# Row maxima of the segment units: whole rows with the causal mask added in VectorE's reduction, in place of blocks with separately masked diagonals

## The chip, the cores and the metric

The kernel runs on one core of a Trainium2 chip. The metric is the device time of one execution in microseconds (us), from the first to the last instruction of the program with what lies around them. The core's engines work side by side and in order, each on its own queue: TensorE (PE in the profile; PEld is its loading of weights), VectorE (DVE), ScalarE (ACT), GpSimd (POOL) and SyncE (SP, which here only issues transfers).

## The reference

Two attentions over the same sequence length (2048 tokens, 512 features, 32 heads of 16) are mixed by a gate. Cut to what matters:

```python
# side A: full softmax attention, no mask
scores = einsum("bhqd,bhkd->bhqk", q, k) * scale
p = softmax(scores); o = einsum("bhqk,bhkd->bhqd", p, v);  a = o @ wo
# side B: four segments of 512 tokens, causal inside a segment, plus a linear memory of earlier ones
mask = (ar[:, None] < ar[None, :]) * (-1e9)
for s in range(4):
    logits = einsum(qs, ks) * scale + mask
    a_dot = softmax(logits) @ vs
    o = g * (phi(qs) @ M) / (phi(qs) @ z + 1e-6) + (1 - g) * a_dot
    M, z = M + phi(ks).T @ vs, z + sum(phi(ks))
b = concat(o) @ wo_b
out = gate * a + (1 - gate) * b          # gate = sigmoid(x . gate_w)
```

The softmax needs, for each query and head, the maximum of its scores before the exponential. This kernel computes these maxima in a pass of products of their own; the change is in that pass, on side B.

## The kernel before

A first stage (to about 327 us) projects x to q, k and v, both sides, and builds the memory terms. The main stage then goes through 64 **units**: a unit is a side, a group of 4 heads and a chunk of 512 queries. A units have 64 slots and B units ("segment units") 10; they alternate, so that a pair has 74 slots, and there are 32 pairs, 2368 slots in all. In every slot `n` of the main stage TensorE does, in this order:

- `score_part(n)` (line 660): one product of up to 512 columns into one of three PSUM banks `st`; ScalarE takes the exponential of it into `p` (line 683).
- `max_part(n + LEAD, bank)` with LEAD = 96 (line 208 through `max_product`): a product into one of four PSUM banks `sm0` to `sm3`, taken in turn, for a unit that comes later; VectorE reduces it to maxima. The list `maxs` says which part each slot does: among the 64 parts of an A unit the 10 parts of a B unit are spread, one every seventh slot (`start, apart = 6, 7`; in the second unit pair and the last one every third slot).
- After every third slot (`BURST = 3`): the products with v of earlier slots (`some_values`, line 716), or products with the output weights in their place (line 793). So TensorE's order of work is three score products and three maximum products in one **burst**, then the products with v, then the next burst; here that is called a **group**.

The score product and the maximum product of a slot use different halves of the array's rows (heads 0 and 1 lie in partitions 0 to 63, heads 2 and 3 from 64), and `maxs` is laid out so that the two of a slot are on opposite halves.

A maximum part on side A is one product of 128 queries by 512 keys for one head and one `tensor_reduce` of the bank (line 223). A B unit needs, for each of 4 heads and 4 blocks `s` of 128 queries, the maximum over the keys up to the query. Before the change its 10 parts are, for each pair `r` of heads:

- `i` = 0 and 1: four products of 128 columns in one bank, the diagonal blocks of two query blocks for two heads. ScalarE copies the bank to `dg` (line 234), GpSimd replaces what lies above the diagonal (line 235), and eight slots later (`MASK_T`) VectorE reduces `dg` (line 238). The bank is free once ScalarE has copied it.
- `i` = 2 and 3: for one head the blocks left of the diagonal of query block 1 (128 columns) and of block 3 (384 columns): two products, one reduction by blocks (line 244).
- `i` = 4: the same of query block 2 for both heads (256 columns each): two products, one reduction (line 248).

In all that is 28 products, each with a load of weights, in 10 slots. `finish_max` then reduces the partial maxima to `nm` (line 180 for A, 182 for B), GpSimd splits it in two (`ms`, lines 187 and 188), and `transpose_max` (lines 196 to 202) turns it on TensorE, copies it on ScalarE and sends it by DMA into rows 48 and 49 of the unit's q, where the score product subtracts it. `todo` and `late` hold the slots at which these steps are issued: the steps of an A unit's `finish_max` are issued right after its last part, its transpose 14 slots after; a B unit's 9 and 18 slots after.

All orders are written out by hand; the waits between engines are put in when the program is built, from the tiles that each instruction reads and writes.

## Time and profile before

| | us |
|---|---|
| median of 3 runs | 1882.21 |
| lowest and highest | 1882.15 and 1885.49 |
| the profiled execution, its own time | 1883.44 |
| its span, first to last instruction | 1881.7 |

TensorE's granted clock is 1.0 of full speed over the span. Busy shares of the span: PE 99%, DVE 85%, ACT 80%, PEld 53%, POOL 17%. In the stretch from 450 to 1700 us the DVE is busy for 1207.2 of 1250 us.

Rows of groups read: line, engine, operation, tiles out<-in, shapes, count | busy us in all, mean ns of one | idle time of the engine just before, and what ended it. Rows of a timeline read: start in us from the span's start, us from the first start to the last end of the merged instructions, engine, line, operation, tiles, count. VectorE's instructions overlap at their ends, so that the next may start before the row's duration is over.

### The profile page before, as it was taken

The page shows a single profiled execution, that of the slowest core. Times are in us where ns is not written, and L with a number is a line of the kernel's source. Part 1 is how long each engine was busy: PE and PEld are TensorE (multiplying, and loading weights), DVE is VectorE, ACT ScalarE, POOL GpSimd, SP SyncE. Part 2 cuts the span into 40 slices and gives each one's busy share as a digit, 9 for nine tenths or more (in the row PEclk, how much of TensorE's full clock was granted, in tenths as well). Part 3 has the DMA queues.
Part 4 walks back from the last instruction along what each step waited for, and adds up shares of the span by engine and source line. Part 5 has one row for each costly group of instructions (what it writes and reads, how often), then busy time and mean ns, then how long its engine had stood idle before and what let it go on. Part 6 is the DMA issues. An engine that isn't in the chain of part 4 may idle for free.

```text
span 1881.7 us, 46459 instructions
## 1 busy us (share of the span) xinstructions
PE 1863.1 (99%) x18153; PEld 1006.1 (53%) x18153; DVE 1596.5 (85%) x2745; ACT 1502.9 (80%) x2900; POOL 314.9 (17%) x515
## 2 busy tenths in 40 slices
PE   9999999999999999999999999999999999999998
PEld 7888676555555454444444444444444454555545
DVE  4235777999999999999999999999999999999820
ACT  5445444898888898888888888888888888888884
POOL 3001222111111111121111111211121211111210
PEclk9999999999999999999999999999999999999999
DMA  7567555234343433343434343434343434343211
GB/s 239 192 231 255 196 184 192 84 115 136 87 109 86 115 91 111 94 117 97 117 92 117 98 113 102 113 98 113 97 113 101 113 103 115 102 114 95 84 57 46
DMA packets 124170, 227.31 MB, mean 121 GB/s; under 512 B 34952, under 2 KB 49960, under 8 KB 123440
## 3 DMA queue, kind: packets, MB, share of 16 engines
q1 hardware_dynamic: 122448, 222.68, 41.1%
q8 instruction: 144, 2.36, 0.5%
q0 software_dynamic: 1216, 1.14, 0.2%
q14 instruction: 74, 0.61, 0.1%
q10 hardware_dynamic: 288, 0.52, 0.1%
HBM read 155.52 MB, written 67.52 MB: 119 GB/s over the span
## 4 chain that ended last, share of the span: by engine, by line
PE 90%; ACT 4%; DMA 3%; DVE 1%; issue 1%; SPq 1%; POOL 1%; ACTq 0%; POOLq 0%; DVEq 0%
PE ops L716 30%; PE st L660 27%; PE sm L208 14%; PE pr L320 11%; PE ops L793 6%; ACT p L683 2%; ACT dg L234 1%; DMA qB<-mt 1%; PE num L502 1%; POOL mn L380 1%; SPq L202 0%; DMA qdB<-q 0%; PE sm L793 0%; PE mps L533 0%; DMA raw<-wqkv 0%
## 5 line engine op out<-in xcount | busy, mean ns | idle before, releaser
L683 ACT ACTIVATE p<-st 128x512 f32<-128x512 f32 x2304 | 1223.4, 605 | 180.8 <-PE sm L208 147.4
L223 DVE TENSOR_REDUCE pm<-sm 128x1 f32<-128x512 f32 x2048 | 1282.9, 683 | 62.1 <-PE sm L208 43.0
L208 PE MATMUL sm<-kA,qA 48*128 48x512 f32 x2048 | 741.5, 445 | 0.0
L660 PE MATMUL st<-qA,kA 50*128 50x512 f32 x2048 | 693.6, 436 | 3.6 <-ACT p L683 3.1
L660 PEld LDWEIGHTS st<-qA,kA 50*128 50x128 f32 x2048 | 332.9, 185 | 436.0 <-ACT p L683 370.6
L716 PE MATMUL ops<-p,vA 128*17 128x512 f32 (+3 forms) x5848 | 556.4, 469 | 0.0
L208 PEld LDWEIGHTS sm<-kA,qA 48*128 48x128 f32 x2048 | 332.5, 184 | 21.1 <-DVE pm L223 7.9
L716 PEld LDWEIGHTS ops<-p,vA 128*17 128x17 f32 x5848 | 109.7, 95 | 174.0 <-issue 152.4
L208 PE MATMUL sm<-kB,qB 48*128 48x128 f32 (+2 forms) x896 | 168.6, 291 | 0.0
L208 PEld LDWEIGHTS sm<-kB,qB 48*128 48x128 f32 x896 | 134.6, 186 | 9.8 <-DVE pm L223 2.8
L235 POOL TENSOR_SCALAR_AFFINE_SELECT dg<-dg 128x512 f32<-128x512 f32 x128 | 81.2, 635 | 289.1 <-ACT dg L234 289.1
L660 PE MATMUL st<-qB,kB 50*128 50x384 f32 (+3 forms) x512 | 120.4, 341 | 2.6 <-DMA qB<-mt 1.2
L187 POOL CAST ms<-nm 128x16 fp32r<-128x16 f32 x64 | 12.6, 196 | 646.6 <-DVE nm L180 401.5
L383 DVE TENSOR_TENSOR q<-full,q 128x512 fp32r<-128x512 f32 x64 | 44.1, 689 | 86.9 <-ACT q L376 86.4
L660 PEld LDWEIGHTS st<-qB,kB 50*128 50x128 f32 x512 | 71.4, 185 | 67.9 <-ACT p L683 47.3
L664 POOL TENSOR_SCALAR_AFFINE_SELECT p<-p 128x512 f32<-128x512 f32 x128 | 78.8, 634 | 95.9 <-ACT p L683 93.9
L244 DVE TENSOR_REDUCE pmB<-sm 128x4 f32<-128x512 f32 x128 | 87.3, 682 | 0.5 <-PE sm L208 0.5
L716 PE MATMUL ops<-p,vB 128*17 128x128 f32 (+3 forms) x1192 | 86.5, 398 | 0.4
L238 DVE TENSOR_REDUCE pmB<-dg 128x4 f32<-128x512 f32 x128 | 86.7, 677 | 0.0
L375 ACT COPY full<-pr 128x512 f32<-128x512 f32 x64 | 37.3, 583 | 52.0 <-PE pr L320 51.8
L234 ACT COPY dg<-sm 128x512 f32<-128x512 f32 x128 | 76.4, 597 | 1.0 <-DVE pmB L238 0.6
L767 DVE RECIPROCAL rec<-rec 128x32 f32<-128x32 f32 x44 | 15.1, 344 | 66.0 <-DMA rec<-odA 35.3
(145 smaller groups left out, 1588.8 us busy)
## 6 DMA issues: line engine op xcount, KB each, us to landing
kA<-kdA SPq DMA_DIRECT2D x256, 128.0 KB
vA<-vdA SPq DMA_DIRECT2D x31, 544.0 KB
kA<-kdA SPq DMA_DIRECT2D x256, 64.0 KB
qdA<-q SPq DMA_DIRECT2D x32, 256.0 KB
kdA<-q SPq DMA_DIRECT2D x32, 256.0 KB
qdB<-q SPq DMA_DIRECT2D x32, 256.0 KB
qA<-qdA SPq DMA_DIRECT2D x64, 128.0 KB
kdB<-q SPq DMA_DIRECT2D x32, 256.0 KB
```

The source lines that it names most:

```text
L208: nc.tensor.matmul(ps[:, n0:n0 + n], rows(qt[u][:, :, s * 128:(s + 1) * 128], h, 48), rows(k[:, :, k0:k0 + n], h, 48), start=True, stop=True)
L223: nc.vector.tensor_reduce(pm[:, h, s, kc:kc + 1], ps, axis=AX.X, op=ALU.max)
L234: nc.scalar.copy(dg, blocked(ps))
L235: nc.gpsimd.affine_select(out=dg, in_=dg, pattern=[[0, 4], [-1, 128]], base=0, channel_multiplier=1, compare_op=ALU.is_ge, fill=MASKED)
L238: todo.append((m + MASK_T, lambda: nc.vector.tensor_reduce(to, dg.rearrange("p (h s) t -> p h s t", h=2), axis=AX.X, op=ALU.max)))
L244: nc.vector.tensor_reduce(pm[:, 1, h, 3:7], blocked(ps), axis=AX.X, op=ALU.max)
L320: nc.tensor.matmul(ps, l(a, k), r(b, k), start=(n == 0), stop=(n == 11))
L660: nc.tensor.matmul(ps[:, n0:n0 + CH - q0], rows(k[:, :, b * 128:(b + 1) * 128], h, 50), rows(q[:, :, q0:], h, 50), start=True, stop=True)
L664: nc.gpsimd.affine_select(out=x, in_=x, pattern=[[0, 4], [1, 128]], base=0, channel_multiplier=-1, compare_op=ALU.is_ge, fill=0.0)
L683: nc.scalar.activation(p[:, h], ps, AF.Exp, scale=SCALE)
L716: nc.tensor.matmul(ops[32 * h:32 * h + 17, q0:q0 + 128 * w], v[:, 17 * h:17 * h + 17], p[:, h, c0:c0 + 128 * w], start=(i == 0), stop=done ...
L793: nc.tensor.matmul(ps[32 * t:32 * t + 32, 128 * (j % (ps.shape[1] // 128)):128 * (j % (ps.shape[1] // 128)) + 128], held[side, c][:, o, 12 ...
```

## The change

A B unit's maxima are taken in whole rows: for a head and a query block `s`, one product over all 128 (s + 1) keys up to and with the diagonal block, and one VectorE instruction that adds a mask, kept in SBUF, takes the smallest of the negated sums, and writes it out as the negated maximum. The mask is zero but for its last 128 columns, in which the part above the diagonal is -3.0e38. So there are 16 products and 16 reductions in place of 28 products, 10 reductions from banks or copies, 4 copies on ScalarE and 4 selects on GpSimd. The 10 slots stay: per pair of heads two slots hold a row block of 128 and one of 384 columns, one slot two of 256, and two slots one of 512. In a slot with two, the order of issue is product, reduction, product, reduction, both in the same bank.

B's `finish_max` no longer reduces, and is issued right after the last part; transposes are issued 8 slots after an A unit's last part and 12 after a B unit's. The mask is built by GpSimd at the start of the main stage, behind the loads of the gates.

```diff
-MASKED = -1.0e9 / SCALE
-MASK_T = 8
...
-    pmB = [mp.tile([128, 2, 4, 8], F32, name=f"pmB{i}", bufs=1) for i in range(2)]
-    for t in pmB:
-        nc.gpsimd.memset(t, -3.0e38)
-
     def finish_max(u):
-        nm = mp.tile([128, 4, 4], F32, tag="nm", name="nm")
-        pm = pmt.pop(u)
+        nm = pmt.pop(u)
         if u[0] == "A":
+            pm, nm = nm, mp.tile([128, 4, 4], F32, tag="nm", name="nm")
             nc.vector.tensor_reduce(nm, pm, axis=AX.X, op=ALU.max, negate=True)
-        else:
-            nc.vector.tensor_reduce(nm.rearrange("p h (a b) -> p (h a) b", b=2),
-                                    pm.rearrange("p b h (a k) -> p (h a) b k", a=2), axis=AX.X, op=ALU.max, negate=True)
...
             k = kt_[u, c]
-            h0 = 2 * r
-            if i < 2:
...
-                dg = dp.tile([128, 4, 128], F32, tag="dg", name="dg")
-                nc.scalar.copy(dg, blocked(ps))
-                nc.gpsimd.affine_select(out=dg, in_=dg, pattern=[[0, 4], [-1, 128]], base=0, channel_multiplier=1,
-                                        compare_op=ALU.is_ge, fill=MASKED)
...
+            for h, s in (((0, 0), (0, 2)), ((0, 1), (1, 1)), ((1, 0), (1, 2)), ((0, 3),), ((1, 3),))[i]:
+                w = 128 * (s + 1)
+                n0 = 128 * (s == 2) + 256 * (s == 1 and h)
+                max_product(ps, u, 2 * r + h, s, n0, w, k)
+                nc.vector.tensor_tensor_reduce(out=tri["rest"][:, 0:w], in0=ps[:, n0:n0 + w], in1=tri["mask"][:, CH - w:],
+                                               scale=-1.0, scalar=3.0e38, op0=ALU.add, op1=ALU.min,
+                                               accum_out=pm[:, 2 * r + h, s:s + 1])
         if m == last_max[u]:
             def finish():
-                late.append((m + MASK_T + 2 + LATE_T - (4 if side == "A" else 0), u, finish_max(u)))
-            todo.append((m + (MASK_T + 1 if side == "B" else 0), finish))
+                late.append((m + LATE_T + (4 if side == "B" else 0), u, finish_max(u)))
+            todo.append((m, finish))
...
+    tri["rest"] = dp.tile([128, CH], F32, name="rest")
+    tri["mask"] = dp.tile([128, CH], F32, name="mask")
+    nc.gpsimd.memset(tri["mask"], 0.0)
+    nc.gpsimd.affine_select(out=tri["mask"][:, 384:], in_=tri["mask"][:, 384:], pattern=[[-1, 128]], base=0, channel_multiplier=1,
+                            compare_op=ALU.is_ge, fill=-3.0e38)
```

More of the change, by code (lines that the diff above doesn't have):

```diff
@@ L167, in gated_mix @@
     pmt = {}
+    tri = {}
     todo = []
     late = []
-    pmB = [mp.tile([128, 2, 4, 8], F32, name=f"pmB{i}", bufs=1) for i in range(2)]
-    for t in pmB:
-        nc.gpsimd.memset(t, -3.0e38)
     def finish_max(u):
-        nm = mp.tile([128, 4, 4], F32, tag="nm", name="nm")
-        pm = pmt.pop(u)
+        nm = pmt.pop(u)
         if u[0] == "A":
+            pm, nm = nm, mp.tile([128, 4, 4], F32, tag="nm", name="nm")
             nc.vector.tensor_reduce(nm, pm, axis=AX.X, op=ALU.max, negate=True)
-        else:
-            nc.vector.tensor_reduce(nm.rearrange("p h (a b) -> p (h a) b", b=2),
-                                    pm.rearrange("p b h (a k) -> p (h a) b k", a=2), axis=AX.X, op=ALU.max, negate=True)
         ms = mp.tile([128, 2, 2, 2, 4], F32R, tag="ms", name="ms")
@@ L202, in transpose_max @@
                 nc.sync.dma_start(raw(qt[u])[64 * r + 48:64 * r + 50], raw(mt)[32 * i + 16 * r:32 * i + 16 * r + 16])
-    def blocked(ps):
-        return ps.rearrange("p (b t) -> p b t", t=128)
     def max_product(ps, u, h, s, n0, n, k, k0=0):
@@ L215, in max_part @@
         if u not in pmt:
-            pmt[u] = mp.tile([128, 4, 4, 4], F32, tag="pmA", name="pm") if side == "A" else pmB[(c * NG + g) % 2]
+            pmt[u] = mp.tile([128, 4, 4] + [4] * (side == "A"), F32, tag="pm" + side, name="pm")
         pm = pmt[u]
@@ L227, in max_part @@
             k = kt_[u, c]
-            h0 = 2 * r
-            if i < 2:
-                for n in range(4):
-                    b = i + 2 * (n % 2)
-                    max_product(ps, u, h0 + n // 2, b, 128 * n, 128, k, 128 * b)
-                dg = dp.tile([128, 4, 128], F32, tag="dg", name="dg")
-                nc.scalar.copy(dg, blocked(ps))
-                nc.gpsimd.affine_select(out=dg, in_=dg, pattern=[[0, 4], [-1, 128]], base=0, channel_multiplier=1,
-                                        compare_op=ALU.is_ge, fill=MASKED)
-                to = pm[:, i, h0:h0 + 2, 3::4] if i == 0 else pm[:, i, h0:h0 + 2, 1::6]
-                todo.append((m + MASK_T, lambda: nc.vector.tensor_reduce(
-                    to, dg.rearrange("p (h s) t -> p h s t", h=2), axis=AX.X, op=ALU.max)))
-            elif i < 4:
-                h = h0 + i - 2
-                max_product(ps, u, h, 1, 0, 128, k)
-                max_product(ps, u, h, 3, 128, 384, k)
-                nc.vector.tensor_reduce(pm[:, 1, h, 3:7], blocked(ps), axis=AX.X, op=ALU.max)
-            else:
-                for f in range(2):
-                    max_product(ps, u, h0 + f, 2, 256 * f, 256, k)
-                nc.vector.tensor_reduce(pm[:, 0, h0:h0 + 2, 4:6], ps.rearrange("p (h b t) -> p h b t", h=2, b=2), axis=AX.X,
-                                        op=ALU.max)
+            for h, s in (((0, 0), (0, 2)), ((0, 1), (1, 1)), ((1, 0), (1, 2)), ((0, 3),), ((1, 3),))[i]:
[5 more added lines that the diff above has]
+                                               accum_out=pm[:, 2 * r + h, s:s + 1])
         if m == last_max[u]:
             def finish():
-                late.append((m + MASK_T + 2 + LATE_T - (4 if side == "A" else 0), u, finish_max(u)))
-            todo.append((m + (MASK_T + 1 if side == "B" else 0), finish))
+                late.append((m + LATE_T + (4 if side == "B" else 0), u, finish_max(u)))
+            todo.append((m, finish))
     def run_todo(m):
@@ L602, in gated_mix @@
     va = ctx.enter_context(tc.tile_pool(name="va", bufs=2, reuse_waits="tile"))
-    dp = ctx.enter_context(tc.tile_pool(name="dp", bufs=3, reuse_waits="tile"))
+    dp = ctx.enter_context(tc.tile_pool(name="dp", bufs=1, reuse_waits="tile"))
     ob = ctx.enter_context(tc.tile_pool(name="ob", bufs=2, reuse_waits="tile"))
```

## The prediction

> **What bounds the kernel now.** I read the page first: busy shares, the slices of the span, the chain that ended last.

> ```profile
> PE 1863.1 (99%) x18153; PEld 1006.1 (53%) x18153; DVE 1596.5 (85%) x2745; ACT 1502.9 (80%) x2900; POOL 314.9 (17%) x515
> PE   9999999999999999999999999999999999999998
> DVE  4235777999999999999999999999999999999820
> PE 90%; ACT 4%; DMA 3%; DVE 1%; issue 1%; SPq 1%; POOL 1%; ACTq 0%; POOLq 0%; DVEq 0%
> ```

> TensorE is never idle and carries 90% of the chain; VectorE is the second nearest, nearly full in the main stage. So a weight load saved is worth something, and so is anything that holds TensorE. How near the two are is read from the timeline, one group of TensorE and then VectorE beside it.

> ```profile
> 829.15 0.50 PE L660 MATMUL st<-qA,kA 50*128 50x512 f32 x1
> 829.15 0.73 PE L208 MATMUL sm<-kA,qA 48*128 48x512 f32 x2
> 829.49 0.63 PE L660 MATMUL st<-qA,kA 50*128 50x512 f32 x2
> 829.73 0.40 PE L208 MATMUL sm<-kA,qA 48*128 48x512 f32 x1
> 830.06 1.05 PE L716 MATMUL ops<-p,vA 128*17 128x512 f32 x8
> 831.04 0.50 PE L660 MATMUL st<-qA,kA 50*128 50x512 f32 x1
> ```
> ```profile
> 829.72 3.85 DVE L223 TENSOR_REDUCE pm<-sm 128x1 f32<-128x512 f32 x6 [0.28 <-PE sm L208]
> ```

> The burst of three slots runs from 829.15 to 830.06, 0.91 us; the group 1.89 us. Slots start at 829.15, 829.49 and 829.73: 0.34 us apart where the load of weights is open, 0.24 where it is hidden. The first product ends at 829.65 and VectorE starts at 829.72: 0.07 us from hand to hand. Its reductions follow at 0.60 us (below: four in 2.48 us, the last 0.68 long). So inside a burst VectorE falls behind: it starts at 829.72, 830.32 and 830.92, and catches up during the products with v. The four banks make that harmless, and the waits view agrees, with 10.7 us in all:

> ```profile
> PEld sm L208 <- DVE pm L223: 10.7, 46, 0.4
> ```

> **Weight loads.** Bursts with each of the three kinds of segment slot:

> ```profile
> 639.37 0.50 PE L660 MATMUL st<-qA,kA 50*128 50x512 f32 x1
> 639.38 0.55 PE L208 MATMUL sm<-kB,qB 48*128 48x128 f32 x3
> ...
> 640.49 0.84 PE L716 MATMUL ops<-p,vA 128*17 128x384 f32 x8
> 641.26 0.50 PE L660 MATMUL st<-qA,kA 50*128 50x512 f32 x1
> ...
> 642.46 0.84 PE L716 MATMUL ops<-p,vA 128*17 128x384 f32 x8
> ```
> ```profile
> 802.39 0.50 PE L660 MATMUL st<-qA,kA 50*128 50x512 f32 x1
> ...
> 802.97 0.45 PE L208 MATMUL sm<-kB,qB 48*128 48x128 f32 x2
> 803.34 1.05 PE L716 MATMUL ops<-p,vB 128*17 128x512 f32 x8
> ```
> ```profile
> 864.16 0.50 PE L660 MATMUL st<-qA,kA 50*128 50x512 f32 x1
> ...
> 864.50 0.28 PE L208 MATMUL sm<-kB,qB 48*128 48x256 f32 x1
> ...
> 864.62 0.28 PE L208 MATMUL sm<-kB,qB 48*128 48x256 f32 x1
> ...
> 865.06 1.05 PE L716 MATMUL ops<-p,vA 128*17 128x512 f32 x8
> ```

> Four products of 128 columns make the burst 1.12 us, 0.21 over the plain one; 128 with 384 makes 0.95, two of 256 make 0.90. After the change a unit has the same four slots of 128 with 384 and two of 256, and four of one 512 in place of the four 1.12 us ones: 4 x 0.21 x 32 units = 27 us saved. In a burst that waits for another engine anyway less is saved; I take 24, with 0 and 27 as ends. The columns streamed are the same, 2560 per pair of heads.

> **VectorE's own work.** The rows nearest to the new instruction, which this trace does not have:

> ```profile
> L383 DVE TENSOR_TENSOR q<-full,q 128x512 fp32r<-128x512 f32 x64 | 44.1, 689 | 86.9 <-ACT q L376 86.4
> L467 DVE SCALAR_TENSOR_TENSOR jk<-xg,gw 128x512 f32<-128x512 f32 x16 | 11.0, 688 | 11.1 <-ACT ex L387 11.0
> L771 DVE TENSOR_TENSOR rec<-rec,gA 128x32 f32<-128x32 f32 x16 | 3.1, 192 | 0.6
> ```
> ```profile
> 303.96 0.68 DVE L467 SCALAR_TENSOR_TENSOR jk<-xg,gw 128x512 f32<-128x512 f32 x1
> 304.57 0.08 DVE L467 DVE_READ_ACCUMULATOR jk<-xg,gw 128x1 f32 x1
> 304.69 0.69 DVE L467 SCALAR_TENSOR_TENSOR jk<-xg,gw 128x512 f32<-128x512 f32 x1
> 305.30 0.08 DVE L467 DVE_READ_ACCUMULATOR jk<-xg,gw 128x1 f32 x1
> 305.30 2.48 DVE L223 TENSOR_REDUCE pm<-sm 128x1 f32<-128x512 f32 x4
> ```

> From 192 ns at 32 columns and 689 at 512 a column costs 1.035 ns; so 0.29, 0.42, 0.56 and 0.69 us at 128, 256, 384 and 512, 7.84 us for the 16 of a unit. An instruction with an accumulator is two rows: the read starts 0.61 us after the main one and ends 0.69 after it, and the reduction behind it starts with the read (305.30). If the new ones overlap so, by 0.08 each, they take 6.6 us; if nothing overlaps and each read adds 0.08, 9.1. Before it was 10 x 0.60 + 0.13 for `nm` (the 209 ns of line 182 less the overlap) = 6.1. So VectorE gets 0.5 to 3.0 us more per pair of units; I take 0.5, the value of the row itself. Its load per pair of 74 slots goes from 74 x 0.60 + 0.1 = 44.5 us to 45.0 (47.5 at most). The pair's time now:

> ```profile
> L208 PE MATMUL sm<-kB,qB x896: 218/273/407, 327.7 to 1795.4; 48*128 48x128 f32 x129, 48*128 48x256 f32 x26, 48*128 48x384 f32 x25
> ```

> From the third slot of the main stage to its last but one part are 1467.7 us, 757 groups: 1.94 us each, 47.9 per pair. VectorE alone would still fit; the work term is nothing.

> **The new wait.** This decides. Each slot with two row blocks now issues product, reduction, product, reduction in one bank. Before, one reader came behind all products of a bank. In the changed kernel's built order the second product carries a wait of its own (TensorE's queue, one such slot and what follows):

> ```
> L196 Matmult sm_3170<-kB_193,qB_3417 128x128 [waits DMAHW4_49,DMAHW3_49,DMAHW7_49,DMAHW0_49,DVE_49]
> L196 Matmult sm_3170<-kB_193,qB_3417 128x384 [waits DVE_49]
> L639 Matmult st<-qA_1476,kA_187 128x512 [waits Activation_49]
> ```

> The wait's value is the count that the first reduction's accumulator read raises, in all 128 slots of 128 with 384 and all 64 of two 256; in the kernel before no second product waits for VectorE. VectorE reads in order, so that this reduction comes behind those of the earlier slots of the burst. Behind the waiting product on TensorE's queue stand the rest of the burst and the products with v; ScalarE waits for the scores.

> [...]

> Its price, with the plain burst's times. First product 0.27 us (the median of the tile's row above; 0.28 for 256), second product otherwise 0.06 or 0.12 behind the first (802.97; 864.50 and 864.62):
> - first place in the burst: 829.15 + 0.27 + 0.07, reduction to the end of its read 0.30 (0.43 for 256), 0.07 back: 829.86 in place of 829.21, a stall of 0.65; 0.73 for 256.
> - second place: the reduction can't start before 830.32; 830.32 + 0.37 = 830.69 in place of 829.55, 1.14; 1.21 for 256.
> - third place: 830.92 + 0.37 = 831.29 in place of 829.79, 1.50; 1.57 for 256.

> Segment slots are 7 apart, so the three places come equally often: 1.10 and 1.17 us. Behind a stall a load of weights is open, 0.10 more (0.34 against 0.24). 128 x 1.20 + 64 x 1.27 = 235 us.

> Not all of it is lost. The plain burst at 641.26 took 1.20 us, so TensorE already waits in places, and a stall can take over such a wait. I give back 40; ends 0 and 90. The other way, VectorE is further behind in places than in the plain group:

> ```profile
> 804.47 0.68 DVE L244 TENSOR_REDUCE pmB<-sm 128x4 f32<-128x512 f32 x1
> ```

> That bank's products ended at 802.97 + 0.45 = 803.42, 1.05 us earlier, where the plain third place has 0.9. If VectorE were 0.2 us later everywhere, 192 x 0.2 = 38 us more; if it had always caught up, every stall would cost the first place's price, 130 us in all.

> **What goes at no price.** ScalarE's 128 copies and GpSimd's 128 selects lie on engines that are 80% and 17% busy; in the 1.12 us burst the copy is counted already. Transposes are issued 8 and 12 slots behind the last part, not 14 and 18; 8 slots at 0.65 us are 5 us, against one reduction backlog of about 1 us and short GpSimd steps; if that cover is gone it costs up to some us per unit. The mask is built once.

> **Sum.** Span 1881.7, execution 1883.4, median 1882.2: one us apart, nothing beside these terms. 1882.2 - 24 + 235 - 40 = 2053 us.

> **Rivals.**
> - *The wait is hidden, the loads count:* 1882 - 24 = 1858. It decides if a slot with two blocks loses under 24 / 192 = 0.125 us. Against it: even in first place the stall is 0.65. For it: only that VectorE has time left.
> - *Shallow stalls:* VectorE has mostly caught up, and TensorE's old waits take over much: 1882 - 27 + 130 - 30 = 1955.
> - *The new instruction runs at half rate:* the first reduction takes 0.13 or 0.27 us more, 128 x 0.13 + 64 x 0.27 = 34; VectorE's work grows by 5120 columns, 5.3 us per pair, to 50.3 us of about 53 (2053 for 1882 of 47.9), of which I let a quarter show, an estimate: 1.3 x 32 = 42 more, 2129. Against it: line 467 reads two fp32 tensors, accumulates, and takes 688 ns beside 689 without. [...]

> **How the numbers follow.** The forecast, with its ends 1985 (50 us less of stall and 20 more given back) and 2115 (38 us more stall, nearly nothing given back, loads worth little), has 0.78; shallow stalls below 1985 have 0.10, half rate or worse above 2115 0.07, the hidden wait 0.04, no change 0.01. So 1985 to 2115 holds about 8 in 10. A measurement of this kernel tells 0.2%, 4 us, from no change: faster 0.04, same 0.01, slower 0.95.

> **What would show it.** In the profile after: TensorE's waits for the new instruction at the maximum products, some 192, near 1 us each in place of 10.7 us in all, by place in the burst 0.65, 1.1 and 1.5; bursts with one 512 at 0.91; busy shares of VectorE and ScalarE down, `dg` gone; the new rows at 0.29 to 0.69 us with reads of 0.08. Wrong it would be if these waits total under 60 us, or if VectorE were full throughout.

## The result and the profile after

| | before | after |
|---|---|---|
| median, us | 1882.2 | 2146.48 |
| lowest and highest, 4 runs each | 1882.15 and 1885.49 | 2144.28 and 2149.26 |
| the profiled execution, its span | 1881.7 | 2147.5 |
| TensorE's mean granted clock | 1.0 | 0.954 |

The kernel became slower by a factor of 1.14 [1.1379, 1.1421], 264 us. The prediction was 2053 us, 1985 to 2115: right in direction and in the wait that does most of it, too low by 93 us and outside its range.

The page after, the same parts as before: busy shares, the slices, the granted clock, the chain.

```profile
PE 1956.1 (91%) x17769; PEld 988.1 (46%) x17769; DVE 1636.9 (76%) x3417; ACT 1462.3 (68%) x2772; POOL 236.4 (11%) x387
PE   9999998889888888999998899998888888888899
DVE  4236776888878878888888878878888888888830
PEclk9999997999988979999999989989999999999999
PE 49%; DVE 45%; issue 2%; DMA 2%; ACT 2%; POOL 1%; SPq 0%; DVEq 0%; POOLq 0%; ACTq 0%
```

TensorE has 384 products fewer and is no longer full: 91% in place of 99%. VectorE is no fuller either (76%, before 85%), and yet it carries 45% of the chain, before 1%. The two engines take turns: each idles while the other ends the chain. The waits view (engine, tile and line, what it waits for: us in all, count, longest) has the turns:

```profile
PEld sm L196 <- DVE pm L220: 249.1, 193, 2.4
PE sm L196 <- DVE pm L220: 174.3, 185, 2.3
DVE pm L211 <- PE sm L196: 156.6, 195, 2.4
DVE rest L220 <- PE sm L196: 102.9, 195, 0.8
```

The first row was 10.7 us, for another reader, in the kernel before. There are 192 slots with two row blocks, and TensorE's loads wait 193 times, 1.29 us each. (The second row is the same stall seen by the products behind those loads; the two aren't added.) VectorE in its turn waits 195 times for the second product. One such slot, third in its burst, from the timeline of TensorE and then of VectorE:

```profile
1001.56 0.50 PE L639 MATMUL st<-qA,kA 50*128 50x512 f32 x1
1001.56 0.73 PE L196 MATMUL sm<-kA,qA 48*128 48x512 f32 x2
1001.90 0.39 PE L639 MATMUL st<-qA,kA 50*128 50x512 f32 x1
1002.12 0.24 PE L196 MATMUL sm<-kB,qB 48*128 48x128 f32 x1
1002.13 0.39 PE L639 MATMUL st<-qA,kA 50*128 50x512 f32 x1
1003.67 0.43 PE L196 MATMUL sm<-kB,qB 48*128 48x384 f32 x1 [1.16 <-DVE pm L220]
1004.04 1.05 PE L695 MATMUL ops<-p,vA 128*17 128x512 f32 x8
```
```profile
1000.85 2.57 DVE L211 TENSOR_REDUCE pm<-sm 128x1 f32<-128x512 f32 x4
1003.33 0.28 DVE L220 CUSTOM_DVE_ANT_0 rest<-sm,mask 128x128 f32<-128x128 f32 x1
1003.54 0.08 DVE L220 DVE_READ_ACCUMULATOR2_ANT pm<- 128x1 f32 x1
1004.15 0.56 DVE L220 CUSTOM_DVE_ANT_0 rest<-sm,mask 128x384 f32<-128x384 f32 x1 [0.53 <-PE sm L196]
```

The product of 128 columns is done by 1002.36, but VectorE still has the two reductions of the slots before to do and comes to it at 1003.33, 1.77 us after the burst's start: just the prediction's 830.92 - 829.15. The read of the accumulator ends at 1003.62, the second product starts at 1003.67. The burst takes 2.48 us (1001.56 to 1004.04) where a plain one takes 0.91. The groups have the new instruction:

```profile
L220 DVE CUSTOM_DVE_ANT_0 rest<-sm,mask 128x512 f32<-128x512 f32 x128 | 87.2, 682 | 0.9 <-PE sm L196 0.7
L220 DVE CUSTOM_DVE_ANT_0 rest<-sm,mask 128x384 f32<-128x384 f32 x128 | 71.4, 558 | 70.6 <-PE sm L196 70.6
L220 DVE CUSTOM_DVE_ANT_0 rest<-sm,mask 128x256 f32<-128x256 f32 x128 | 53.8, 420 | 35.1 <-PE sm L196 31.6 <-PE st L639 3.5
L220 DVE CUSTOM_DVE_ANT_0 rest<-sm,mask 128x128 f32<-128x128 f32 x128 | 36.2, 283 | 5.7 <-PE st L639 5.6
L220 DVE DVE_READ_ACCUMULATOR2_ANT pm<- 128x1 f32 x512 | 42.6, 83 | 0.0
```

0.28, 0.42, 0.56 and 0.68 us, reads of 0.08: the times that were forecast. The instruction is not slower than expected.

What the prediction has no word of is the clock. It is seen in windows of 3.41 us (stretch, its length, busy time and instructions of PE, PEld, DVE, ACT and POOL, granted clock, DMA share, GB/s), two places of the main stage:

```profile
480.61:484.03 3.42, 2.15 (x19) 0.75 (x20) 2.88 (x8) 1.78 (x5) 0.80 (x1) 1.00 0.76 186
484.03:487.44 3.41, 3.41 (x26) 1.42 (x22) 1.86 (x5) 1.82 (x5) 0.48 (x1) 0.50 0.02 10
487.44:490.86 3.42, 2.26 (x31) 1.08 (x27) 2.62 (x7) 2.14 (x5) 0.00 (x0) 1.00 0.26 71
1002.85:1006.27 3.42, 2.60 (x21) 0.94 (x23) 2.02 (x7) 1.53 (x4) 0.00 (x0) 1.00 0.41 118
1006.27:1009.68 3.41, 2.27 (x26) 0.89 (x18) 3.34 (x8) 2.92 (x6) 0.00 (x0) 1.00 0.00 0
1009.68:1013.09 3.41, 3.41 (x15) 1.07 (x17) 1.72 (x4) 1.09 (x2) 0.00 (x0) 0.50 0.02 5
1013.09:1016.51 3.42, 3.42 (x16) 0.99 (x18) 1.89 (x3) 1.67 (x4) 0.64 (x1) 0.50 0.00 0
1016.51:1019.92 3.41, 2.48 (x45) 1.95 (x47) 2.07 (x6) 2.14 (x4) 0.00 (x0) 1.00 0.20 77
```
```profile
1011.02 1.91 PE L695 MATMUL ops<-p,vA 128*17 128x512 f32 x8
```

The windows in which TensorE was busy 2.15 and 2.27 of 3.41 us are followed by one and two at half clock; there eight products with v take 1.91 us, not 1.05. The granted clock in this trace is 1.00 or 0.50 and nothing between, in 31 stretches each. A mean of 0.954 over 2147.5 us is then 2 x 0.046 x 2147.5 = 198 us at half clock; the stretches at 0.50 add up to 196 us of the span. For other runs the time at half clock is an estimate, worked out from their mean clock in the same way.

### The profile page after: what moved, and what is told of

The parts are those of the page before. It is cut to its first block, busy times and chain, and to the rows that moved or that the text cites. A ratio compares the mean times of both kernels' runs of the same rounds, so it can differ in the third digit from the quotient of the medians.

```text
span 2147.5 us, 45769 instructions
## 1 busy us (share of the span) xinstructions
PE 1956.1 (91%) x17769; PEld 988.1 (46%) x17769; DVE 1636.9 (76%) x3417; ACT 1462.3 (68%) x2772; POOL 236.4 (11%) x387
## 3 DMA queue, kind: packets, MB, share of 16 engines
q0 software_dynamic: 1216, 1.14, 0.2%
## 4 chain that ended last, share of the span: by engine, by line
PE 49%; DVE 45%; issue 2%; DMA 2%; ACT 2%; POOL 1%; SPq 0%; DVEq 0%; POOLq 0%; ACTq 0%
DVE pm L211 37%; PE ops L695 12%; PE st L639 12%; PE pr L293 9%; PE sm L196 8%; DVE rest L220 5%; PE ops L772 5%; PE sm L772 1%; DMA raw<-xT 1%; POOL mn L353 1%; ACT p L662 1%; DVE rec L746 0%; PE num L475 0%; DMA vs<-wqkv 0%; PE mt_ps L187 0%
## 5 line engine op out<-in xcount | busy, mean ns | idle before, releaser
L196 PE MATMUL sm<-kA,qA 48*128 48x512 f32 x2048 | 760.7, 462 | 0.0
L639 PE MATMUL st<-qA,kA 50*128 50x512 f32 x2048 | 708.2, 446 | 0.0
L695 PE MATMUL ops<-p,vA 128*17 128x512 f32 (+3 forms) x5848 | 583.0, 489 | 0.0
L639 PEld LDWEIGHTS st<-qA,kA 50*128 50x128 f32 x2048 | 341.2, 192 | 445.6 <-ACT p L662 348.2
L196 PE MATMUL sm<-kB,qB 48*128 48x128 f32 (+3 forms) x512 | 196.0, 383 | 182.3 <-DVE pm L220 174.3
L196 PEld LDWEIGHTS sm<-kA,qA 48*128 48x128 f32 x2048 | 347.5, 194 | 15.2 <-issue 7.1
L220 DVE CUSTOM_DVE_ANT_0 rest<-sm,mask 128x128 f32<-128x128 f32 (+3 forms) x512 | 248.7, 486 | 112.3 <-PE sm L196 102.9
L196 PEld LDWEIGHTS sm<-kB,qB 48*128 48x128 f32 x512 | 97.3, 190 | 251.2 <-DVE pm L220 248.9
L639 PE MATMUL st<-qB,kB 50*128 50x384 f32 (+3 forms) x512 | 124.8, 361 | 0.0
L356 DVE TENSOR_TENSOR q<-full,q 128x512 fp32r<-128x512 f32 x64 | 44.5, 695 | 87.0 <-ACT q L349 87.0
L639 PEld LDWEIGHTS st<-qB,kB 50*128 50x128 f32 x512 | 79.1, 208 | 66.2 <-ACT p L662 53.3
L772 PE MATMUL ops<-woA,vA 128*32 128x128 f32 x1664 | 70.7, 291 | 0.0
L772 PE MATMUL ops<-woB,vB 128*32 128x128 f32 x1664 | 67.4, 281 | 0.0
L293 PE MATMUL pr<-xh,wql 128*128 128x512 f32 x128 | 54.5, 425 | 0.7 <-ACT xh L406 0.4
```

The source lines that it names most:

```text
L196: nc.tensor.matmul(ps[:, n0:n0 + n], rows(qt[u][:, :, s * 128:(s + 1) * 128], h, 48), rows(k[:, :, k0:k0 + n], h, 48), start=True, stop=True)
L220: nc.vector.tensor_tensor_reduce(out=tri["rest"][:, 0:w], in0=ps[:, n0:n0 + w], in1=tri["mask"][:, CH - w:], scale=-1.0, scalar=3.0e38, op ...
L293: nc.tensor.matmul(ps, l(a, k), r(b, k), start=(n == 0), stop=(n == 11))
L356: nc.vector.tensor_sub(q2, full, q1.bitcast(F32))
L639: nc.tensor.matmul(ps[:, n0:n0 + CH - q0], rows(k[:, :, b * 128:(b + 1) * 128], h, 50), rows(q[:, :, q0:], h, 50), start=True, stop=True)
L695: nc.tensor.matmul(ops[32 * h:32 * h + 17, q0:q0 + 128 * w], v[:, 17 * h:17 * h + 17], p[:, h, c0:c0 + 128 * w], start=(i == 0), stop=done ...
```

## The experiments

The theory after the result: **the second product's wait for the first reduction in its bank** is all of it, directly and through the clock. Rivals: the new instruction or the whole rows cost VectorE's time; or the wait costs what was predicted and something else the rest. Times of before beside these runs were 1882.2 to 1884.8; ratios are against those.

**Both products, then both reductions** (everything else as changed):

```diff
-            for h, s in (...)[i]: max_product(...); tensor_tensor_reduce(...)
+            for h, s, w, n0 in at_: max_product(ps, u, 2 * r + h, s, n0, w, k)
+            for h, s, w, n0 in at_: nc.vector.tensor_tensor_reduce(...)
```

> The changed kernel with one thing undone: in a slot with two row blocks both products are issued first, then both reductions. Theory (the second product waits for the first reduction in its bank): that wait is gone, TensorE's waits at the segment products are under 15 us, the granted clock is 1.00, and the time is 1850 to 1875, 10 to 30 under the kernel before. Rival (the new instruction or the 16 reductions hold VectorE, and TensorE with it): still over 2050.

Measured: 1856.54, ratio 0.9858 [0.9841, 0.9874], clock 1.0. From its page, then from its waits:

```profile
PE 1845.8 (100%) x17769; PEld 987.4 (53%) x17769; DVE 1609.2 (87%) x3417; ACT 1446.2 (78%) x2772; POOL 236.5 (13%) x387
```
```profile
PEld sm L196 <- DVE pm L211: 14.1, 53, 0.6
PEld sm L196 <- DVE pm L221: 2.0, 8, 0.3
```

The same instructions in another order: the 193 waits are 8, and TensorE is full again. The order of issue costs 2146.5 - 1856.5 = 290 us; the rest of the change gains 26.

**The kernel before, with only the order changed**: in its parts with two products each reduction comes right behind its product (shown for 128 with 384 columns; two of 256 likewise); loads, copies and masks as before.

```diff
                 max_product(...128 columns...)
+                nc.vector.tensor_reduce(pm[:, 1, h, 3:4], ps[:, 0:128], axis=AX.X, op=ALU.max)
                 max_product(...384 columns...)
-                nc.vector.tensor_reduce(pm[:, 1, h, 3:7], blocked(ps), axis=AX.X, op=ALU.max)
+                nc.vector.tensor_reduce(pm[:, 1, h, 4:7], blocked(ps[:, 128:]), axis=AX.X, op=ALU.max)
...
```

> The kernel before with the wait alone added: its slots of 128 with 384 and of two 256 columns issue product, reduction, product, reduction with the plain reductions; diagonal copies and 28 loads stay. Theory (the wait is the cause): some 192 waits of 1.1 to 1.3 us at the segment products, clock below 1, and 2080 to 2170. Rival (the new instruction is the cause): 1885 to 1900, for 192 more short reductions on VectorE.

Measured: 2181.75 (2 runs), ratio 1.1583 [1.156, 1.1607], clock 0.965; above what was expected.

```profile
PEld sm L208 <- DVE pmB L243: 171.9, 128, 2.1
PEld sm L208 <- DVE pmB L249: 93.9, 64, 2.3
```

192 waits again, 1.38 us each, with plain reductions and nothing else of the change: the wait, with 192 short reductions more on VectorE, makes such a kernel some 300 us slower. The new instruction and the whole rows aren't needed for it.

**The waits filled with products that nobody reads**, one or three of 512 columns ahead of each second product. The stall's length is kept, but TensorE is busy in it: from the start of a bank's first product to the start of its second are 1.34 us (128 with 384) and 1.47 (two of 256) in the changed kernel, 1.36 and 1.48 with three unread products (means of the trace's starts).

```diff
+                if n0 and m >= LEAD:
+                    for _ in range(3):          # 1 in the other kernel
+                        max_product(banks[free[0]], u, 2 * (1 - r) + h, s, 0, CH, k)
                 max_product(ps, u, 2 * r + h, s, n0, w, k)
```

> The changed kernel with three more products of 512 columns issued ahead of each second product of a bank, in the main stage: their results, in the bank of the next slot, are read by nobody and overwritten. They take about 0.75 us of a wait that lasted 0.98 us or more. Theory (the half-clock stretches cost time beside the waits): the clock comes back to 0.98 or more, and the time falls to 2060 to 2115 although TensorE does more. Rival (the low clock lies where TensorE waits and costs nothing): the time stays at 2140 to 2160 whatever the clock does. Second rival (the products don't fit into the wait): over 2160.

> The changed kernel with one unread product of 512 columns in each wait, in place of three. If the granted clock follows how much TensorE works in a stretch, the clock lies between 0.954 and 0.994 and the time between 2090 and 2146, 2105 to 2135. Rival (it takes a wait filled to the end, or the time of the filled run came from something else): 2140 to 2155.

| products in each wait | mean clock | at half clock, worked out as above, us | median, us |
|---|---|---|---|
| 0 (the changed kernel) | 0.954 | 198 | 2146.5 |
| 1 | 0.963 | 158 | 2132.7 |
| 3 | 0.994 (0.985 in the second run) | 25 (63) | 2089.8 |

```profile
core 0: 2081.1 us, clock 0.994
```
```profile
PEld sm L196 <- DVE pm L223: 127.5, 193, 1.8
```

Of the kernel with three, the clock, and the row of these waits. A kernel with 576 products more, of no use, is 57 us faster (2089.8, 2082.86 to 2096.77, 2 runs): the time at half clock is nearly gone. So of the 290 us at least 57 are the clock, and at most 2089.8 - 1856.5 = 233 the stalls themselves. Two estimates of the clock's whole share agree with that bound. In the changed kernel's trace, from 328 to 2060 us, one score product after another took 0.685 us at full clock and 0.975 at half clock; 200 of them fell into 195 us at half clock, 200 x 0.29 = 58 us. And the two profiled executions are 2147.5 - 2081.1 = 66 us apart for 198 - 25 = 173 us at half clock, 0.38 us each, so 76 for 198. The clock is then some 58 to 76 us and the stalls 214 to 232.

**Each row block in a bank of its own**, the order kept, product, reduction, product, reduction:

```diff
+                if s == 2 or (s == 1 and h):
+                    ps = bank()
-                n0 = 128 * (s == 2) + 256 * (s == 1 and h)
+                n0 = 0
```

> The changed kernel with its order of product, reduction, product, reduction, but each row block in a bank of its own, so that a slot with two takes two of the four banks in turn. Theory (the wait comes from sharing the bank): no wait for the first reduction, and 1855 to 1895, some waits for a bank read three parts earlier. Rival (the order alone makes the wait, whatever the bank): 2100 to 2150.

Measured: 1889.19, ratio 1.0032 [1.0021, 1.0043].

```profile
PEld sm L196 <- DVE pm L211: 42.4, 150, 0.9
```

The wait for the new instruction is gone with the shared bank, but for 7 times and 2.4 us. Six more banks per unit in the ring of four are taken sooner than VectorE gives them back: 150 waits of 0.28 us for a reduction three parts back, where the order with both products first has 53. It is 33 us behind that one, more than the 26 that the rest of the change gains.

**What the 26 us are made of.** Six kernels take the parts singly: with both products first, a second scratch tile for the sums that nobody reads; the products split again into 28, with one scratch tile and with two; plain reductions without the mask; and, in the kernel before, one product in place of the four diagonal ones, or no copies and selects.

```diff
-    tri["rest"] = dp.tile([128, CH], F32, name="rest")
+    tri["rest"] = [dp.tile([128, CH], F32, name=f"rest{i}") for i in range(2)]   # used in turn
```

> Products first, then reductions, as in the run with products first (1856.5), and the reductions write their unused sums to two scratch tiles in turn, so that a second reduction in a slot need not wait for the first on VectorE itself (0.1 us, 192 times). Theory (TensorE bounds, VectorE has time left): 1852 to 1857. Rival (VectorE is close enough that its 20 us show): 1840 to 1850.

> Products first, then reductions, but each row block above 128 columns is made by two products, the diagonal block by itself: 28 products and loads of weights as in the kernel before, the rest as changed. Theory (the 26 us gained with products first come from the loads): 1876 to 1888. Rival (they come from ScalarE's 128 copies and GpSimd's selects, which are gone here too): 1854 to 1862.

> The version with two scratches (1842.3) with 28 products and loads in place of 16. With one scratch the 12 more loads cost 7 us. Theory (there VectorE's own wait hid part of what the loads cost TensorE; a burst with four loads in one slot is 1.12 us with and without ScalarE's copy): 1858 to 1868, some 20 us. Rival (the loads are worth 7 us whatever VectorE does, and the rest of the gain over the kernel before came with the copies): 1847 to 1852.

> Products first, then 16 plain reductions of the bank in place of the new instruction: no mask is read or added (the maxima take in the part above the diagonal, which this leaves out of the computation) and no accumulator is read. Theory (the new instruction costs VectorE little and TensorE nothing): 1850 to 1858. Rival (the second operand and the accumulator read cost time that shows): 1835 to 1848.

> The kernel before with the loads alone changed: each slot of four diagonal blocks makes one product of 512 columns instead of four of 128, 16 loads and not 28; copies, selects and reductions stay as they are (the maxima of the diagonal blocks are those of other blocks, so that part of the computation is left out). Theory (loads are worth what the pair with two scratches showed, 8.6 us): 1870 to 1878. Rival (in the kernel before they are worth the 24 us of the prediction, and the copies nothing): 1855 to 1862.

> The kernel before with ScalarE's copies and GpSimd's selects alone taken away: VectorE reduces the bank of the four diagonal blocks itself, in the slot (the mask is left out of the maxima); 28 loads and 10 reductions stay. Theory (what the loads don't explain of the 40 us between the kernel before and two scratches comes from the copies on ScalarE): 1848 to 1862. Rival (ScalarE has room, the copies cost nothing): 1877 to 1885.

| kernel | median, us | ratio to before |
|---|---|---|
| both products first | 1856.54 | 0.9858 [0.9841, 0.9874] |
| and 28 loads | 1863.51 | 0.99 [0.9885, 0.9914] |
| and two scratch tiles, 16 loads | 1842.31 | 0.979 [0.9775, 0.9804] |
| and two scratch tiles, 28 loads | 1850.92 | 0.983 [0.9816, 0.9845] |
| and plain reductions, no mask | 1839.31 | 0.977 [0.9754, 0.9787] |
| before, 16 loads | 1879.65 | 0.9978 [0.9969, 0.9988] |
| before, no copies, no selects | 1853.36 | 0.9839 [0.9824, 0.9853] |

Read by differences: the 384 loads saved are worth 7.0 (1863.5 - 1856.5), 8.6 (1850.9 - 1842.3) or, in the kernel before, 2.6 to 5.1 us (1879.65 against 1882.2 or the 1884.76 beside it). The theories that went before these runs missed in five of the six, the kernel before without copies being the exception. The 28 loads stayed under theirs with one tile (1876 to 1888) and with two (1858 to 1868), and the kernel before with 16 loads stayed above (1870 to 1878): the loads are cheaper than was thought. Two scratch tiles and the plain reductions fell below theirs (1852 to 1857 and 1850 to 1858): time saved on VectorE shows in the whole. The one scratch tile costs 14.2 us; how, is seen in VectorE's timeline, with one tile and then with two:

```profile
1013.34 0.28 DVE L221 CUSTOM_DVE_ANT_0 rest<-sm,mask 128x128 f32<-128x128 f32 x1
1013.55 0.08 DVE L221 DVE_READ_ACCUMULATOR2_ANT pm<- 128x1 f32 x1
1013.66 0.56 DVE L221 CUSTOM_DVE_ANT_0 rest<-sm,mask 128x384 f32<-128x384 f32 x1
```
```profile
1010.34 0.28 DVE L222 CUSTOM_DVE_ANT_0 rest<-sm,mask 128x128 f32<-128x128 f32 x1
1010.55 0.08 DVE L222 DVE_READ_ACCUMULATOR2_ANT pm<- 128x1 f32 x1
1010.55 0.55 DVE L222 CUSTOM_DVE_ANT_0 rest<-sm,mask 128x384 f32<-128x384 f32 x1
```

With two tiles the second instruction starts with the first one's read, at 1010.55; with one, 0.11 us later, when the read is over: nobody reads the sums, but the second instruction writes where the first one wrote. The program carries this wait: as built with one tile, each of the 192 second instructions waits for the count that the read ahead of it raises; with two, none does. 192 pairs at 0.11 us are 21 us of VectorE's time, of which 14 show.

The mask and the sum themselves cost 1842.3 - 1839.3 = 3 us (a plain reduction writes no scratch tile either, so the kernel with two is the one to compare). And the copies and selects, "at no price" in the prediction, cost 29 to 31 us (1853.36 against 1882.2 or 1884.76). The waits of the kernel before show a part of where, beside those of the kernel without copies:

```profile
PEld st L660 <- ACT p L683: 417.8, 730, 0.9
PEld st L660 <- ACT dg L234: 21.4, 36, 0.9
```
```profile
PEld st L655 <- ACT p L678: 431.3, 778, 0.9
```

TensorE's score product waited for ScalarE, which was copying the diagonal blocks and not taking an exponential: 36 times, 21.4 us, a row that stood in the trace of before. It is not the whole price, and not a sum to add: these loads wait 439 us for `p` and `dg` with copies, and 431 for `p` without. Group by group (from one group's first maximum product to the next one's) the main stage is 1468 us long with copies and 1439 without, and 70 of its 756 groups, longer by over 0.2 us each, make up 27 of those 29 us. One is at 842.50, 2.68 us in place of 2.19: ScalarE copies `dg` first and only then `oraw`, the result of products with v, and the output products wait 0.67 us for it in place of 0.18. So a copy costs at whatever comes behind it on ScalarE; how the 29 to 31 us divide among those places isn't shown.

**The copies put back** into the kernel with both products first and plain reductions:

```diff
+            if i < 2:
+                nc.scalar.copy(dp.tile([128, CH], F32, tag="dg", name="dg", bufs=1), ps)
```

> The version with plain reductions (1839.3; it leaves the mask out of the maxima) with ScalarE's 128 copies of a bank put back, four in each segment unit, into a tile that nobody reads. Theory (ScalarE has room, the copies lie beside other work): 1839 to 1845. Rival (the copies delay the exponentials, and TensorE with them): 1850 to 1860.

Measured: 1903.28, ratio 1.0112 [1.0095, 1.0129], 64 us over the kernel without and above both ranges.

```profile
DVE pm L223 <- ACT dg L221: 57.3, 104, 1.0
PEld st L640 <- ACT dg L221: 10.7, 22, 0.9
```

This doesn't price the copies. VectorE's reductions now wait for ScalarE, 104 times and 57.3 us, although both only read the bank. The price is that of the kernel before without copies.

**The best version** is the change with both products first and two scratch tiles: 1842.31, 2.1% faster than the kernel before and 14% than the changed one.

```profile
PE 1833.0 (99%) x17769; PEld 971.4 (53%) x17769; DVE 1598.4 (87%) x3417; ACT 1445.5 (78%) x2772; POOL 236.4 (13%) x387
```
```profile
PEld sm L196 <- DVE pm L211: 7.1, 23, 0.7
PEld sm L196 <- DVE pm L222: 0.5, 2, 0.3
```

## Why the prediction was wrong in size, step by step

- **The new wait, right.** 192 waits, of the new instruction, at the maximum products. By place in the burst the second product of 128 with 384 starts 1.05, 1.30 and 1.66 us behind the first, for two of 256 1.32, 1.36 and 1.73 (means of the trace's starts). Less what it is behind in the kernel with both products first, place by place, the stalls are 0.89, 1.22, 1.56 and 1.09, 1.21, 1.55; forecast, with the open load, 0.75, 1.24, 1.60 and 0.83, 1.31, 1.67. In second and third place the forecast is right to 0.12, a little long; in the first the stall is longer by 0.14 and 0.26, although the second product is there 0.16 and 0.22 us behind anyway, not the 0.06 and 0.12 that the prediction took for all three. In sum 128 x 1.23 + 64 x 1.29 = 240 us against 235. This alone would have given 2058. (The 0.9 us that the prediction took for the plain third place is 0.79 by its own rows, 829.73 + 0.40 to 830.92; it went into the range alone.)
- **The step that failed: the clock, a term that the sum doesn't have.** At least 57 us, 58 to 76 by the estimates above. The prediction took all rows at the granted clock of 1.0 that the page of before had throughout, and asked what a stall moves, not what it does to the rate of everything behind it.
- **"Not all of it is lost", 40 us, mis-sized.** At nearly full clock the waits cost at most 233 of those 240, so that at least 7 come back; by the estimates of the clock it is 8 to 26. TensorE of the kernel before was idle for 1881.7 - 1863.1 = 18.6 us in all, which fits: there was little that a stall could take over.
- **Weight loads, 24 us, mis-sized; copies at no price, wrong.** 3 to 9 and 29 to 31 us. The 0.21 us by which the burst of 1.12 us is longer are the loads' own: in the kernel with both products first and 28 loads, which copies nothing, such bursts still take 1.11 us in the median. But a burst shortened is not a kernel shortened: of 27 us 3 to 9 are left, and what takes the rest wasn't found. The copies cost in other places than the burst that they were looked for in: at score and output products that wait for what ScalarE does behind a copy. One row of the trace of before, 21.4 us, pointed there, and the prediction did not read it.
- **VectorE's work is nothing: right for the instruction, 3 us; the one scratch tile, 14 us, wasn't seen.** In the changed kernel it doesn't show: there the second instruction waits longer for its product (1003.62 to 1004.15 above). That the gains come to 26 us, where 24 stood, is luck: two wrong terms and one overlooked cancel. By parts, - 7 - 30 + 3 + 14 = - 20; some 6 us are not assigned to any of them.
- **Sum,** with the clock at its least: 2053 + 5 (the waits) + 33 (give-back, 7 and not 40) + 57 (clock) - 2 (gains) = 2146. A larger share of the clock means as much more given back.
- **Rivals.** The hidden wait and half rate fell with the rows above. Shallow stalls fell too: VectorE had not caught up, 240 us and not 130. The range's upper end took in 38 us of deeper stalls; the clock had no share in it. VectorE's and ScalarE's busy shares fell as was said, though VectorE's busy time grew by 40 us; bursts with one 512 take 0.908 us in the median, 0.91 forecast.

## What to carry to other kernels

Where a bank takes several products, issue them all before the first reader: with product and reduction in turn TensorE waited here for all that stood ahead of that reader on its engine, 1.3 us and not the 0.3 of one small reduction, and the order alone cost 290 us. Price a stall of a full TensorE twice, once as time and once as the clock that it may lose (here 0.954 in place of 1.0, at least 57 us of the 290), and look in the trace for half-clock windows where stalls are many (here 192 from 328 to 2060 us, one in 9 us). What a copy on a busy engine costs is looked for at those who wait for that engine's next instructions, not in the engine's busy share (here 29 to 31 us, with ScalarE 80% busy).

## What the runs showed of the hardware

**An unread result is not free, by the program's waits.** Where two instructions of VectorE in a row write the same scratch tile, the second started 0.11 us later than with two tiles in turn, behind the wait that the program carries for it. What the engine would do without that wait is not shown.
